# Causal masks carried in the shift operands, expert tables worked out in PSUM, and matmuls of zeros at the start

## The chip, the cores and the metric

One core of a Trainium2 chip runs the whole program. Five engines take instructions in their own order: PE (TensorE: matmuls, with weight loads listed apart as PEld), DVE (VectorE), ACT (ScalarE), POOL (GpSimd) and SP, which here only starts DMAs. The metric is the device time of one execution in microseconds (us). "Granted clock" is the share of full speed at which TensorE was let run: 1.00 is 2.4 GHz, 0.50 is 1.2 GHz.

## The reference

Attention with a decay, and then a layer of eight experts of which each token takes one:

```python
# q, k, v: 8 batches x 8 heads x 576 positions x 64; f: 8 x 8 x 576
scores = matmul(q, k.T) / sqrt(64)
cum = cumsum(log(clip(f, 1e-4, 1)), axis=-1)
scores = where(causal, -1e9, scores + cum[..., :, None] - cum[..., None, :])
attn = exp(scores - scores.max(-1));  attn /= attn.sum(-1) + 1e-9
x = matmul(attn, v)                       # as 4608 tokens x 512
logits = x @ w_gate + modality_bias[modality_id]
e = argmax(logits); gate = softmax(logits)[e]
out = gate * (relu(x @ w1[e]) @ w2[e])    # w1: 8 x 512 x 1024, w2: 8 x 1024 x 512
```

## The kernel before

**Attention** runs over 32 pairs of heads (four pairs are one batch). A pair lies in one tile `X` (two heads of 64 partitions each), as a rounded part `X[:,0]` and the rest `X[:,1]`, so that a product is three matmuls. The two heads of a pair use the upper and the lower 64 rows of the PE array; each matmul of a group therefore comes twice. The steps of pair p, by the names that the planner uses:

- `mm(p,g)` (`max_mm`, L525 on): query by key scores from the rounded parts alone, into one of three PSUM buffers `ps`. A bf16 matmul adds the decay of the key (`Cq` by `Sk`, L546), and ahead of it small matmuls of an identity (`id2`) by a triangle of minus 1e30 (`after`, L540) mask the blocks on the diagonal. `mr(p,g)` on DVE takes the row maxima; `sp`, `ssp` and `so` turn them round on PE, split them on DVE and put them, negated, as rows of `Sq` by two DMAs of SP (L586).
- `s(p,g)` (`scores`, L589 on): the scores proper, keys on the partitions. Mask matmuls again (`id2` by `later`, L606), then the shift (`Sk` by `Sq`, bf16, L613: minus the maximum of the query, plus the decay), then three matmuls of `X` (L621). `e` (exp) and `h` (rounding) are ACT's, `r` (the rest, L663) POOL's and DVE's.
- `w(u)`, `d(u)` for head u: attention by v (L689 to L691), and the division on DVE. `kg` (L491) is the gate's product with v.
- `hi`, `lo` split X on ACT and POOL; `cum` (L412) copies the three bf16 parts of the pair's decay into rows of `Sk` by one DMA of SP. `Sk`, `Sq` and `X` have three slots, which pairs take in turn.

**Routing** per batch (`rt`, `sc`): argmax, ranks within the experts, and scatter of the tokens with indirect DMAs to lists in DRAM. After batch 5, `early` (L1327) counts the tokens per expert so far, and works out on DVE, with 25 small instructions, nearly all on SBUF tiles of one partition (L1000 to L1074), which expert the first four tiles of 256 tokens belong to, so that their loads can start before attention ends.

**The experts** (`Moe.run`) take 18 tiles of 256 tokens and a few of 128, PE without a break; the other tables are worked out by `other_tables` in the middle of the third tile.

**The order** in attention is written down by a planner: `Plan.order` takes, among the steps that are ready and whose buffers are free, the one of the least due time; due times are 43.41 us per batch and a table `DUE` of offsets by step, stage (first, second, middle, last batch) and pair. Each engine then runs its instructions strictly in that order.

**The start** (`setup`): constants on DVE and POOL, the decay's sum (`chl`, three bf16 parts), the first two pairs' loads. `setup2` makes the constants for routing.

Of the kernel before, what the change touches and what calls it, by code (L numbers as in the profile page):

```python
# [24 lines left out]
S = 576  # L25
# [30 lines left out]
BIG = 1.0e30  # L56
# [5 lines left out]
def f32(ap):  # L62
# [6 lines left out]
    ('setup2',): ((-7.6276,),), ('gs',): ((-27.0565,),),  # L69
    ('hi',): ((-64.9614, -0.5129, 9.9233, 25.1464,), (-37.0423, -34.3266, 3.0090, 3.2864,), (-169.6259, -130.5347, 3.9150, -109.9118,), (-15.1432, -125.2677, 14.8978, 18.2475,),),  # L70
    ('lo',): ((-30.4199, -46.7722, 10.3081, -40.1680,), (-2.3325, -25.1233, 8.8097, -14.1207,), (-7.8613, -11.7188, 13.3481, 20.8245,), (-10.1281, -19.8797, 18.8280, 34.3170,),),
    ('cum',): ((-242.6133, -50.2149, -6.6544, -25.4361,), (-56.0267, -77.1295, -25.7943, 18.3990,), (-19.3542, -20.5147, -34.8776, -48.3972,), (-31.7442, -27.2763, -26.2392, 12.4635,),),
# [8 lines left out]
    ('ssp',): ((-1.1033, 5.5259, 26.1725, 29.0023,), (8.9962, 9.7417, -25.8497, 38.9986,), (0.8838, 13.9798, 19.4950, 37.8791,), (11.5482, 4.7540, 36.4772, 37.2843,),),  # L81
# [1396 lines left out]
```

## Time and profile before

| what | value |
|---|---|
| three runs, median (lowest to highest) | 850.12 us (849.7 to 854.04) |
| the profiled execution | 849.61 us, its span from first to last instruction 847.8 us |
| PE busy over the span | 807.1 us (95%) |
| attention, about 0 to 376 us; experts, about 376 to 848 us | |

The profile comes from one execution. A busy engine is one with an instruction in flight; for PE, whose matmuls are pipelined, the distance from the start of one group of matmuls to the start of the next is the better measure of what a group costs. A wait is put down to the instruction whose end released it.

### The profile page before, as it was taken

How to read it: one execution, taken by the hardware profiler on the slowest of the kernel's cores; microseconds unless marked ns; L12 is line 12 of the kernel's file. 1: busy time of each engine (PE TensorE's matmuls, PEld its weight loads, DVE VectorE, ACT ScalarE, POOL GpSimd, SP SyncE). 2: the span in 40 equal slices, each digit the busy share in tenths (PEclk: the TensorE clock that was granted, in tenths of full speed). 3: DMA queues.
4: the chain of work that ended last, by engine and by line, in shares of the span. 5: the costliest groups of instructions: out<-in, count | busy, mean ns of one | idle time of the engine just before them, and what ended most of it. 6: DMA issues, size and time to landing. Idle time of an engine off the chain costs nothing.

```text
span 847.8 us, 23444 instructions
## 1 busy us (share of the span) xinstructions
PE 807.1 (95%) x9693; PEld 726.9 (86%) x9693; DVE 627.7 (74%) x1170; ACT 543.2 (64%) x688; POOL 378.7 (45%) x370
## 2 busy tenths in 40 slices
PE   3899999999999999699999999999999999999994
PEld 2689898989898988588999999999999999999873
DVE  8679798989898989877777856666655666566484
ACT  4597889898989897474643654444454445444484
POOL 9386889898989897575433111111000110111110
PEclk9699999999999999899999999999999999999997
DMA  5434353535353533171474731101113421116481
GB/s 171 145 104 140 125 182 116 184 116 180 119 182 116 184 115 108 64 244 58 149 249 157 295 121 51 51 27 49 38 51 137 149 67 50 51 44 207 146 299 30
DMA packets 43016, 107.48 MB, mean 127 GB/s; under 512 B 5391, under 2 KB 5583, under 8 KB 42896
## 3 DMA queue, kind: packets, MB, share of 16 engines
q1 hardware_dynamic: 36192, 84.82, 30.1%
q0 software_dynamic: 6704, 21.02, 6.8%
q8 instruction: 80, 1.31, 0.7%
q14 instruction: 40, 0.33, 0.1%
HBM read 143.14 MB, written 21.80 MB: 195 GB/s over the span
## 4 chain that ended last, share of the span: by engine, by line
PE 86%; DVE 7%; POOL 2%; issue 2%; ACT 1%; DMA 0%; DVEq 0%; POOLq 0%; ACTq 0%
PE ph L1211 23%; PE py L1237 23%; PE ps L621 9%; PE pb L491 4%; PE po L689 4%; PE po L691 3%; PE po L690 3%; PE ps L551 3%; PE ps L613 3%; PE ps L546 2%; PE ph L1293 2%; PE ps L606 2%; PE px L1194 2%; PE ps L540 2%; DVE w1l L1157 1%
## 5 line engine op out<-in xcount | busy, mean ns | idle before, releaser
L1242 POOL DMA_INDIRECT out_dram<-y,xg x36 | 48.0, 1334 | 333.7 <-DVE y L1241 304.8
L1211 PE MATMUL ph<-xh,w1h 128*128 128x256 f32 x576 | 163.3, 284 | 0.3 <-DVE hl L1215 0.3
L1211 PE MATMUL ph<-xl,w1h 128*128 128x256 f32 x576 | 163.1, 283 | 0.0
L1211 PE MATMUL ph<-xh,w1l 128*128 128x256 f32 x576 | 162.9, 283 | 0.0
L663 POOL TENSOR_TENSOR Pl<-Pt,Ph 128x1024 f16<-128x1024 f32 (+1 forms) x63 | 142.0, 2260 | 17.9 <-ACT Ph L651 14.4
L1157 DVE TENSOR_TENSOR w1l<-raw,w1h 128x1024 fp32r<-128x1024 f32 x78 | 97.6, 1265 | 61.5 <-ACT w1h L1155 61.5
L1174 ACT CAST w2h<-raw 128x1024 fp32r<-128x1024 f32 x72 | 74.6, 1048 | 95.1 <-issue 55.3
L1155 ACT CAST w1h<-raw 128x1024 fp32r<-128x1024 f32 x80 | 82.5, 1048 | 82.5 <-PE ph L1211 62.5
L1175 DVE TENSOR_TENSOR w2l<-raw,w2h 128x1024 fp32r<-128x1024 f32 x72 | 87.5, 1221 | 58.7 <-ACT w2h L1174 56.9
L1211 PEld LDWEIGHTS ph<-xh,w1h 128*128 128x128 f32 x576 | 110.5, 192 | 1.2 <-DVE hl L1215 0.5
L1237 PE MATMUL py<-w2h,hh 128*128 128x512 f32 x288 | 111.3, 395 | 0.0
L1211 PEld LDWEIGHTS ph<-xl,w1h 128*128 128x128 f32 x576 | 110.5, 192 | 0.7
L1211 PEld LDWEIGHTS ph<-xh,w1l 128*128 128x128 f32 x576 | 110.5, 192 | 0.0
L1237 PE MATMUL py<-w2l,hh 128*128 128x512 f32 x288 | 110.2, 391 | 0.0
L1237 PE MATMUL py<-w2h,hl 128*128 128x512 f32 x288 | 109.9, 391 | 0.0
L621 PE MATMUL ps<-X 64*128 64x288 f32 (+4 forms) x1152 | 109.8, 319 | 0.0
L689 PE MATMUL po<-vh,Ph 128*128 128x73 f16 x930 | 100.3, 199 | 2.1 <-DVE lgh L705 2.1
L403 POOL TENSOR_TENSOR X<-raw,X 128x1152 fp32r<-128x1152 f32 x32 | 84.7, 2649 | 38.5 <-ACT X L397 38.2
L691 PE MATMUL po<-vh,Pl 128*128 128x73 f16 x930 | 99.8, 198 | 1.5 <-DVE Pl L663 1.3
L690 PE MATMUL po<-vl,Ph 128*128 128x72 f16 x930 | 100.1, 196 | 0.0
L689 PEld LDWEIGHTS <-Ph 128*128 128x128 f16 x960 | 93.6, 98 | 5.9 <-issue 2.8
L636 ACT ACTIVATE Pt<-ps,lnp 128x576 f32<-128x576 f32 (+1 forms) x96 | 81.3, 864 | 24.9 <-PE ps L621 24.9
(301 smaller groups left out, 1944.2 us busy)
## 6 DMA issues: line engine op xcount, KB each, us to landing
raw<-in_w_dram SPq DMA_DIRECT2D x84, 1024.0 KB
raw<-in_qk_dram SPq DMA_DIRECT2D x32, 608.0 KB
vT<-in_vt_dram SPq DMA_DIRECT2D x32, 320.0 KB
xg<-xs SPq DMA_DIRECT2D x18, 514.0 KB
vr<-in_v_dram SPq DMA_DIRECT2D x30, 256.0 KB
raw1b<-in_w_dram SPq DMA_DIRECT2D x4, 1024.0 KB
hxg<-xs SPq DMA_DIRECT2D x5, 257.0 KB
vr<-in_v_dram SPq DMA_DIRECT2D x8, 128.0 KB
```

The lines of the kernel that those rows point to most:

```text
L403: e.tensor_tensor(self.two(X[:, 1]), self.two(self.get("raw", p)), self.two(f32(X[:, 0])), ALU.subtract)
L621: nc.tensor.matmul(ps[:, h, c0:c0 + w], X[r, x, k], X[r, y, q], start=False, stop=(j == 2), skip_group_check=True)
L636: nc.scalar.activation(self.get("Pt", (p, i))[:, :, o:o + w], ps[:, :, 0:w], AF.Exp, bias=self.lnp, scale=0.125)
L663: e.tensor_tensor(self.Pl_t[p % 2][:, :, c], self.exps(p, i), self.Ph_t[p % 2][:, :, c], ALU.subtract)
L689: nc.tensor.matmul(o, Ph[:, c0:c0 + P], vh[:, c, hh, :], start=(c == 0), stop=False)
L690: nc.tensor.matmul(o[:, 1:73], Ph[:, c0:c0 + P], vl[:, c, hh, :], start=False, stop=False)
L691: nc.tensor.matmul(o, Pl[:, c0:c0 + P], vh[:, c, hh, :], start=False, stop=(c == ic))
L1155: x = nc.scalar.copy(self.w1h[a], self.raw1[i][a])
L1157: y = e.tensor_tensor(self.w1l[a], self.raw1[i][a], f32(self.w1h[a]), ALU.subtract)
L1175: y = nc.vector.tensor_tensor(self.w2l[a], self.raw2[a], f32(self.w2h[a]), ALU.subtract)
L1211: y = nc.tensor.matmul(ph[:, i, :], w[:, k, f0:f0 + P], x[:, k, :], start=(j == 0), stop=(j == len(m) - 1))
L1237: x = nc.tensor.matmul(py, h[:, k, c * P:c * P + P], w[:, k, :], start=(j == 0), stop=(j == len(m) - 1))
```

## The change

- **Masks.** The mask matmuls go, with `id2`, `after` and `later`. The shift matmuls carry the mask in rows of their operands that were empty: `Sk` has three variants per slot (no mask, and one for each half of a diagonal block), `Cq` too, and `Sq` holds a staircase (`ques`) next to the shift's rows. A shift matmul over a diagonal block is cut into pieces of 64 columns, each with its variant.
- **The decay's rows** go to three variants, so `cum` is now two DMAs of SP (one per head), read from a copy in DRAM (`sums`) that SP writes once; for pair 0 it is six DMAs, three on ACT's queue. The operands of slots 1 and 2 are filled by two new steps, `slot`, on ACT and POOL.
- **Early tables.** They are worked out in the PSUM bank of the counts, in two pieces with a DVE step of routing between, and with fewer instructions; the count of what is done (four instructions) moves to `other_tables` in the source. The loads that follow are a step of their own, `early3`.
- **Zeros.** 24 matmuls of 512 columns of zeros stand ahead of the first step, and 56 of 256 columns behind nine of the first steps. They write a PSUM bank that the first `w` takes over.
- **Order and constants.** A new `DUE` table, planner's costs for `mm` and `s` lowered, `setup2` cut in three, and the constants of the experts moved from the program's start behind it.

```diff
-BIG = 1.0e30
+BEFORE = (24, 512)
+BETWEEN = {('gs',): 16, ('mm', 0, 2): 5, ('mm', 0, 1): 10, ('mm', 1, 2): 7, ('v1', 0): 3, ('v3', 0): 2, ('s', 0, 2): 7, ('kg', 0, 1): 3,
+           ('mm', 2, 2): 3}
+MLOW, MTOP = 2.0 ** -43, 2.0 ** 36
...
-    ('setup2',): ((-7.6276,),), ('gs',): ((-27.0565,),),
+    ('slot',): ((0.0000, -90.2608, -60.5121,),), ('setup2',): ((-42.1805,),), ('setup3',): ((-15.4352,),),
...
+        self.idle = self.new(self.ps_o, "po", -1, [P, 512], F32, 1)
+        self.turn_over(*BEFORE)
...
+    def rows(self, copy, i):
+        copy(self.Sk[:, i].rearrange("p v (c n) -> p v c n", n=P),
+             self.keys.rearrange("p v (o n) -> p v o n", o=1).broadcast_to([P, 3, NJ, P]))
...
     def put_cum(self, p):
 
         self.own(("cum", p % 3), p)
-        self.nc.sync.dma_start(self.Sk[3:114:22, p % 3, 0:S], self.chl[2 * p:2 * p + 2])
+        for h, e in enumerate((self.nc.sync, self.nc.scalar if p == 0 else self.nc.sync)):
+            o, u = self.Sk[64 * h + 3:64 * h + 6, p % 3, :, 0:S], 2 * p + h
+            if p:
+                e.dma_start(o, self.sums[u].rearrange("r (o s) -> r o s", o=1).broadcast_to([3, 3, S]))
+            else:
+                for v in range(3):
+                    e.dma_start(o[:, v], self.chl[u:u + 1])
+        if p == 0:
+            self.nc.sync.dma_start(self.sums, self.chl)
...
+    def parted(c0, w, ic, j0):
+
+        if j0 + w != MW[ic]:
+            return [(c0, w, ic, j0, 0, 0)]
+        e = w - 64
+        r = [(c0 + e, 64, ic, j0 + e, 1, 2)]
+        if w > 64:
+            r = [(c0 + e - 64, 64, ic, j0 + e - 64, 2, 1)] + r
+        return ([(c0, w - P, ic, j0, 0, 0)] if w > P else []) + r
...
-                    nc.tensor.matmul(ps[:, h, c0:c0 + n], self.id2[r, x], self.later[r, x, 0:n], start=first, stop=False,
-                                     skip_group_check=True)
-                first = False
+        parts = []
         for c0, w, c, i0 in segs:
+            n = 0
+            if i0 == P * c:
+                n = min(w, P)
+                parts += [(c0 + 64 * a, 64, c, i0 + 64 * a, 1 + a) for a in range(n // 64)]
+            if w > n:
+                parts.append((c0 + n, w - n, c, i0 + n, 0))
+        for n, (c0, w, c, i0, v) in enumerate(parts):
...
-            add("early", (), [("PE", 0.2), ("POOL", 0.15), ("DVE", 4.5), ("SP", 2.3)], 0, early, (), [("sc", EB, c) for c in range(NJ)], take=("pb", "e"), free=[("pb", "e")])
+            add("early", (), "PE", 0.25, self.begin_early, (early,), [("setup4",), ("rt", EB, 4)], take=("pb", "e"))
+            add("early1", (), "DVE", 2.0, self.go_early, (), [("early",)])
+            add("early2", (), "DVE", 1.8, self.go_early, (), [("early1",)], free=[("pb", "e")])
+            add("early3", (), "SP", 2.3, self.load_early, (), [("early2",)] + [("sc", EB, c) for c in range(NJ)])
...
+    def turn_over(self, n, w):
+
+        for _ in range(n):
+            self.nc.tensor.matmul(self.idle[:, 0:w], self.none[:, 0:P], self.none[:, 0:w], start=True, stop=True)
...
             for s in self.steps(early).order():
                 s["fn"]()
+                self.turn_over(BETWEEN.get(s["name"], 0), 256)
```

PE in the steady part, one group of scores `s(p,0)` (288 columns, of which the first 128 lie on the diagonal). Before, `id` by `later` is the mask and `Sk` by `Sq` the shift:

```order
L606 LDWEIGHTS id_173
L606 MATMUL ps<-later,id_173 128x128
...
L606 MATMUL ps<-later,id_173 128x64
...
L613 LDWEIGHTS Sk
L613 MATMUL ps<-Sq,Sk 128x288
...
L621 MATMUL ps<-X_117 128x288 x6
```

Two mask blocks (192 columns per head) stand ahead of one shift of 288. PE in the same group in the changed kernel:

```order
L646 LDWEIGHTS Sk
L646 MATMUL ps<-Sq,Sk 128x64
...
L646 MATMUL ps<-Sq,Sk 128x64
...
L646 MATMUL ps<-Sq,Sk 128x160
...
L654 MATMUL ps<-X_101 128x288 x6
```

The mask's columns are gone; the shift's 288 columns come as 64, 64 and 160, each with its own weights.

DVE at the early tables before (`c_na` are the counts, `c_ea` and `c_ka` the expert and the place of each tile, `c_taba` the table, `pb` a PSUM bank):

```order
L739 TENSOR_REDUCE rei<-rc 128x5
L1000 COPY c_na<-pb 1x8
L1007 TENSOR_SCALAR c_nia<-c_na 1x8
...
L1026 TENSOR_TENSOR c_lea<-c_cuma,c_io 1x32
...
L1059 CAST c_taba<-c_cuma 1x1
...
L1072 TENSOR_SCALAR c_done<-c_done 1x8
L1073 TENSOR_TENSOR c_done<-c_done,c_nta 1x8
L1074 TENSOR_SCALAR c_done<-c_done 1x8
L663 TENSOR_TENSOR Pl_214<-ps,Ph_212 128x2x512
L561 TENSOR_REDUCE mt<-ps 128x2 x2
```

The rest of the exponentials (L663) and the next maxima (L561) stand behind the whole chain. DVE at the same place in the changed kernel:

```order
L1405 CAST pb<-pb 1x8
L1406 TENSOR_SCALAR pb<-pb 1x8
...
L1416 TENSOR_TENSOR c_le_8474<-pb,c_io 1x32
...
L772 TENSOR_REDUCE rei<-rc 128x5
L1421 TENSOR_TENSOR c_le_8475<-c_io,pb 1x4
...
L1433 COPY c_early<-pb 1x16
L1130 TENSOR_TENSOR c_done<-c_early 1x8
L1131 TENSOR_SCALAR c_done<-c_done 1x8
...
L595 TENSOR_REDUCE mt<-ps 128x2 x2
L696 TENSOR_TENSOR Pl_212<-ps,Ph_210 128x2x512
```

Every instruction of the tables has a PSUM operand; routing's minimum (L772) now stands in the middle. In the order that results the four instructions of `c_done` (on SBUF) still stand at this place, ahead of the maxima (L595), which now come before the rest (L696).

PE at the start before (`gmax` is the gate's scale, then the first maxima of pair 0):

```order
L467 MATMUL pb<-ident,gmax 1x128
L470 MATMUL pb<-gmax_232,ones_209 128x1
L540 LDWEIGHTS id_173
L540 MATMUL ps<-after,id_173 128x64
...
L546 MATMUL ps<-Sk,Cq 128x64
```

PE starts with two small matmuls and goes on to the first pair. PE at the start of the changed kernel (`none` is the tile of zeros):

```order
L947 LDWEIGHTS none
L947 MATMUL po<-none 128x512
...
L498 MATMUL pb<-ident,gmax 1x128
L501 MATMUL pb<-gmax_265,ones_224 128x1
L947 LDWEIGHTS none
L947 MATMUL po<-none 128x256
...
L569 MATMUL ps<-Sk,Cq 128x64
```

24 matmuls of zeros stand ahead of the first step and 16 narrower ones between it and the first pair; the steps themselves keep their order here.

## Rows read from the trace of the kernel before

**Rows 1.** Stages: us, busy of PE, PEld, DVE, ACT, POOL, PEclk, DMA share, GB/s.
```profile
60.00:304.00 244.00, 242.34 (x4872) 218.78 (x4869) 211.54 (x524) 213.51 (x276) 205.14 (x179) 1.00 0.46 148
304.00:376.00 72.00, 63.56 (x1274) 56.73 (x1272) 58.69 (x151) 53.63 (x67) 53.60 (x56) 0.95 0.36 121
376.00:848.00 472.00, 459.15 (x2960) 416.31 (x2956) 313.02 (x397) 236.71 (x295) 80.47 (x79) 0.99 0.33 114
```
**Rows 2.** Waits from 60 to 304 us: total, times, longest.
```profile
ACT ps L630 <- PE ps L621: 12.8, 17, 1.2
ACT Pt L636 <- PE ps L621: 11.7, 17, 1.8
```
**Rows 3.** Timeline of PE, one pair's matmuls: start us, us, engine, line, operands, count.
```profile
282.10 0.34 PE L540 MATMUL ps<-after,id 64*128 64x128 bf16 x8
282.28 0.38 PE L546 MATMUL ps<-Sk,Cq 64*128 64x192 bf16 x4
...
285.07 0.26 PE L606 MATMUL ps<-later,id 64*128 64x128 bf16 x4
285.17 0.29 PE L613 MATMUL ps<-Sq,Sk 64*128 64x288 bf16 x2
...
286.36 0.29 PE L606 MATMUL ps<-later,id 64*128 64x128 bf16 x6
286.48 0.38 PE L613 MATMUL ps<-Sq,Sk 64*128 64x448 bf16 x4
```
**Rows 4.** Groups by line on PE, 60 to 304 us: count, busy us, mean ns.
```profile
L606 PE MATMUL ps<-later,id 64*128 64x64 bf16 (+1 forms) x410 | 20.3, 205 | 0.0
```
**Rows 5.** Stages at the start, as in rows 1.
```profile
21.00:24.00 3.00, 0.86 (x7) 0.24 (x3) 2.79 (x7) 0.00 (x0) 3.00 (x2) 0.85 0.00 1
...
30.00:33.00 3.00, 3.00 (x26) 2.63 (x26) 2.46 (x5) 1.28 (x2) 0.00 (x0) 0.50 0.38 104
39.00:42.00 3.00, 2.08 (x32) 1.46 (x28) 2.75 (x5) 3.00 (x5) 3.00 (x2) 1.00 0.79 277
```
**Rows 6.** Timeline at the start: loads on SP, work on DVE, then PE.
```profile
0.82 0.61 SPq L247 DMA_DIRECT2D Pt<-in_f_dram  x1
...
3.68 0.73 DVE L274 TENSOR_SCALAR Pt<-Pt 64x576 f32<-64x576 f32 x1 [0.83 <-DMA Pt<-in_f_dram]
...
13.72 0.37 PE L467 MATMUL pb<-ident,gmax 128*1 128x128 f32 x1 [13.72 <-POOL vh L329]
...
27.25 0.38 PE L606 MATMUL ps<-later,id 64*128 64x128 bf16 x4
```
**Rows 7.** Timeline of PE, the end of the first pair's scores.
```profile
38.06 0.34 PE L540 MATMUL ps<-after,id 64*128 64x128 bf16 x8
```
**Rows 8.** Timeline at the early tables, DVE and POOL.
```profile
340.03 0.14 DVE L1000 COPY c_na<-pb 1x8 f32<-1x8 f32 x1
340.21 0.88 DVE L1007 TENSOR_SCALAR c_nia<-c_na 1x8 int32<-1x8 f32 x1
...
341.65 2.63 POOL L403 TENSOR_TENSOR X<-raw,X 128x1152 fp32r<-128x1152 f32 x1
...
341.79 2.53 DVE L1026 TENSOR_TENSOR c_lea<-c_cuma,c_io 1x32 f32<-1x32 f32 x1
...
346.32 2.32 DVE L1072 TENSOR_SCALAR c_done<-c_done 1x8 f32<-1x8 f32 x1
...
348.95 1.23 DVE L663 TENSOR_TENSOR Pl<-ps,Ph 128x1024 f16<-128x1024 f32 x1
```
**Rows 9.** Timeline of PE behind the early tables.
```profile
350.23 0.50 PE L606 MATMUL ps<-later,id 64*128 64x128 bf16 x8 [4.98 <-DVE Pl L663]
```
**Rows 10.** The stage behind the early tables, as in rows 1.
```profile
350.00:355.00 5.00, 4.53 (x54) 3.54 (x54) 3.19 (x12) 2.16 (x2) 0.33 (x2) 0.58 0.23 82
```
**Rows 11.** Timeline of SP's queue in the steady part.
```profile
66.49 0.67 SPq L412 DMA_DIRECT2D Sk<-chl  x1
67.95 1.21 SPq L586 DMA_DIRECT2D Sq<-mT  x2
```

More of the change, by code (lines that the diff above doesn't have):

```diff
@@ L292, in setup @@
-        mask(self.after, 1)
+        self.queries(nc.gpsimd.tensor_copy, 0)
+        self.Ph_t = [t([P, 2, PW], F16, f"Ph{i}") for i in range(2)]
+        self.Pl_t = [t([P, 2, PW], F16, f"Pl{i}") for i in range(2)]
+        for x in self.vh:
+            nc.gpsimd.memset(x[:, :, :, 0:1], 1.0)
+            nc.gpsimd.memset(x[64:128, 4, :, 0:1], 0.0)
+        for x in self.Ph_t + self.Pl_t:
+            nc.gpsimd.memset(x[:, :, 1600:], 0.0)
         nc.scalar.activation(ft, ft, AF.Ln)
+        self.rows(nc.scalar.copy, 0)
@@ L304, in setup @@
         nc.scalar.activation(one, one, AF.Exp)
[L305 to L310 removed]
+        for x in self.X3:
+            nc.vector.memset(f32(x[:, :, S:QC]), 0.0)
         nc.sync.dma_start(self.idt, ids.bitcast(I32).rearrange("p (n o) -> p n o", o=2))
@@ L933, in __init__, with constants @@
         nc = self.nc
+        self.xg, self.xh, self.xl = {}, {}, {}
+        self.xgh, self.xhh, self.xlh = {}, {}, {}
+        self.rings, self.used = {}, {}
+        self.ring("xg", keep, 3, [P, 2, 514], F32)
+    def constants(self):
+        nc, keep = self.nc, self.keep
         self.ident = keep.tile([P, P], F32, name="cident")
@@ L947, in __init__ @@
         self.gap = keep.tile([1, 1], I32, name="c_gap")
-        self.xg, self.xh, self.xl = {}, {}, {}
-        self.xgh, self.xhh, self.xlh = {}, {}, {}
-        self.rings, self.used = {}, {}
-        self.ring("xg", keep, 3, [P, 2, 514], F32)
+        self.zeros = keep.tile([1, 8], F32, name="c_zeros")
+        nc.gpsimd.memset(self.zeros, 0.0)
     def ring(self, name, pool, n, shape, dt):
@@ L1327, in early, with t @@
     def early(self, acc, pc):
-        self.first_table(self.counts(acc, pc, "a"))
-        for t in range(2):
-            self.load_x(t)
+        self.nc.tensor.matmul(pc[:, 0:8], self.ones, acc, start=True, stop=True)
+        yield
+        vec = self.nc.vector
+        at = 8
+        def t(*shape):
+            nonlocal at
+            n = int(np.prod(shape))
+            at += n
+            x = pc[0:1, at - n:at]
+            if len(shape) == 1:
+                return x
+            return x.rearrange("o (a b) -> o a b", b=shape[1])
@@ new lines, in early @@
+        keep = self.keep.tile([1, 16], F32, name="c_early")
+        s1, s3 = [1, EARLY, 1], [1, EARLY, 8]
+        ni = t(8).bitcast(I32)
+        vec.tensor_copy(ni, pc[0:1, 0:8])
+        vec.tensor_scalar(ni, ni, 8, None, ALU.arith_shift_right)
+        e = t(EARLY + 1, 1)
+        vec.memset(e[:, 0:1], -1.0)
+        at_nt = at
+        nt, cum = t(8), t(1, 8)
+        vec.tensor_copy(nt, ni)
+        vec.tensor_tensor_scan(cum[:, 0], nt, self.zeros, 0.0, ALU.add, ALU.add)
+        io = self.io[:, 0:EARLY]
@@ new lines, in early @@
+        base, k = t(EARLY, 1), t(EARLY, 1)
+        le, left = (self.keep.tile([1, EARLY, n], F32, name=f"c_le{n}") for n in (8, 1))
+        vec.tensor_tensor(le, cum.broadcast_to(s3), io.broadcast_to(s3), ALU.is_le)
+        vec.tensor_reduce(e[:, 1:], le, AX.X, ALU.add)
+        vec.tensor_tensor(le, le, cum.broadcast_to(s3), ALU.mult)
+        vec.tensor_reduce(base, le, AX.X, ALU.max)
+        yield
+        vec.tensor_tensor(left, io, base, ALU.subtract)
+        vec.scalar_tensor_tensor(k, e[:, 1:], float(CAP // T), left, ALU.mult, ALU.add)
@@ L1333, in run @@
+        vec.tensor_copy(keep[:, 0:16], pc[0:1, at_nt:at_nt + 16])
+        self.row = [tab[0:1, :, i:i + 1] for i in range(EARLY)]
+        self.last = ex[:, EARLY:EARLY + 1]
+        self.early_counts = keep
+        yield
+        for i in range(2):
+            self.load_x(i)
+        yield
     def run(self, acc, loads, behind, ahead, ranks):
```

297 lines of the change are left out of this document (154 added, 143 removed), and 54 rows, old and new, of the table DUE.

## The prediction

> **What bounds the kernel now.** I read the stages first, then the waits, the matmuls of one pair in the timeline, and last the two places where PE stands still. The stages [rows 1] show that from 60 to 304 us PE is busy for 242.3 of 244.0 us at full clock, while ACT (213.5), DVE (211.5) and POOL (205.1) have an eighth or more to spare. The longest waits of ACT in that stretch end with PE's scores, 12.8 and 11.7 us [rows 2]. So in the middle of attention PE's stream of matmuls is the bound, and a microsecond taken out of it is a microsecond gained until another engine is full. From 304 to 376 us PE is busy for 63.6 of 72 us only: the longest hole is a wait of 4.98 us that ends with DVE's L663 [rows 9]. At the start PE runs, once it has work, at half clock: 0.50 from 30 to 33 us [rows 5]. From 376 us on the experts keep PE at 459.2 of 472 us, and there the order of the instructions is what it was; I put no change there.
>
> **Masks, what goes.** In one pair there are six groups of mask matmuls, three in the maxima (6, 8 and 4 instructions) and three in the scores (4, 6 and 8). Start to start up to the shift that follows, 8 take 282.28 - 282.10 = 0.18 us, 4 take 0.10 and 6 take 0.12 [rows 3]. That is 0.40 us in the maxima and 0.40 in the scores, 0.80 us per pair. For a check: the groups hold 2 x 832 columns per head, both heads at once, and 1664 / 2.4 GHz is 0.69 us.
>
> **Masks, what comes.** The shift's columns stay as they are, but a diagonal block is cut: 28 pieces per head and pair stand where there were 12, and 18 more of them than before are 64 columns wide. No group of before holds such pieces with the shift's own weights. The mask groups are the nearest: they took 0.80 us for 0.69 us of columns, 0.11 us over, and if that lies with their ten pieces of 64 columns, it is 0.01 us each. 18 x 0.01 = 0.18, which leaves 0.80 - 0.18 = 0.62 us gained per pair, and this value I take. The ends: pieces that cost nothing give 0.80. Pieces that cost a slot each, whatever their width, give 32 added matmuls (16 pieces, two heads) at 0.18 / 8 = 0.022 us, 0.70 us, and leave 0.10.
>
> **How much of it reaches the end.** There are 410 of the scores' mask matmuls between 60 and 304 us [rows 4], 18 per pair: 23 pairs. 23 x 0.62 = 14.3 us. That stretch would then take 230 us, with ACT at 93% and DVE at 92%; both wait for PE now and will wait less, and the first time that one of them is late PE waits in turn. I take nine tenths, 12.8 us (ends: 45%, if ACT and DVE can't be packed so close, and all). The other nine pairs, 5.6 us, run at the start and the end of attention, where other waits set the pace: half, 2.8 us.
>
> **The decay's rows.** One DMA of SP with 0.67 us of issue [rows 11] becomes two per pair. What stands behind them on SP, the next `so` (1.21 us for two) and the loads, starts up to 0.7 us later. `mm` waits for these rows. In the new order the first maxima of every fourth pair stand before a gate product and a group of scores instead of behind them, with `so` and then `cum` on SP ahead: about 1 us on DVE, 1.2 and 1.3 us of issue, and a landing for which the only read row is the first load (issued from 0.82 to 1.43 us, its user starts at 3.68 [rows 6]), 2.25 us. 5.8 us in sum. Between lie the last scores of the pair before, two heads of attention by v and two groups of maxima; by a pair's 244.0 / 23 = 10.6 us I estimate them at 6 us. So it is covered, narrowly, and I cost it at nothing; uncovered it is a fraction of a microsecond in every fourth pair.
>
> **Early tables.** From the first copy (340.03) to L663 (348.95) DVE is 8.9 us on them. Three instructions on SBUF tiles take 0.88, 2.53 and 2.32 us, against 0.14 us for the copy out of PSUM. L1026 ends as POOL's subtraction that began at 341.65 does, 2.63 us later [rows 8]. So it is POOL that they wait for, some 5.3 us in all; the other 22 instructions take the remaining 3.2 us, 0.145 each. In the changed kernel 18 instructions with a PSUM operand take their place. [...]
>
> But in the order that results, the four instructions of `c_done`, still on SBUF, stand at the same place, ahead of the maxima. Of the waits 0.7 and 2.4 us go; the third (about 2.2) may meet POOL anywhere in a subtraction, half of it on the mean. 23 instructions (the 18, the four, and a copy of the last expert) at 0.145 us, 0.2 for routing's minimum and 1.1 of waiting give 4.6 us instead of 8.9: 4.3 us less. Behind the hole the clock was 0.58 on the mean from 350 to 355 us [rows 10], with 4.5 us of work: about 1.9 us lost, of which a shorter hole gives back perhaps half. What is late next is step 4 of routing, which PE now meets before the last scores of its pair; I take 0.7 us off for it. Sum: 4.3 + 0.9 - 0.7 = 4.5 us (ends 2 and 7).
>
> **The start.** The first pair's scores and two gate products run from 27.25 to 38.06 us [rows 6, 7] at a clock of 0.50; at full clock a stream of matmuls would take half, 5.4 us less. Before that PE was nearly idle (0.86 of 3 us from 21 to 24 us, clock 0.85 and falling [rows 5]). The zeros fill such waits. 40 matmuls of 256 columns stand between the pairs; 256 columns at 2.4 GHz are 0.11 us, 4.3 us together, and PE has to do them in order even when its next step is ready. The waits of before cover most of that. ACT takes over as the bound from 39 us on, where it is busy for 3.00 of 3 us [rows 5], but its work starts earlier too. The first matmul of a step stood at 13.72 us [rows 6]; with six DMAs for the first rows, three of them behind ACT's table load, I leave the first maxima where they are. I take 4.5 us (ends 0, if zeros and ACT eat it, and 6).
>
> [...]
>
> **Sum.** 12.8 + 2.8 + 4.5 + 4.5 = 24.6 us. The profiled execution took 849.6 us, near the median of 850.1; 849.6 - 24.6 = 825.0 us.
>
> **Rivals.** (a) ACT and DVE become the bound: for it speaks that ACT is at 88% and DVE at 87% now, with dependent steps on a ring of three PSUM buffers; against it, that most of their idle time is waiting for PE. Then 45% of the steady gain is had, 6.4 us, of the edges 1.4, of the start 4.5 and of the tables 4.5: 849.6 - 16.8 = 832.8. (b) The matmul's slot, not its columns, is what is paid: 0.10 us per pair, 23 x 0.10 + 0.4 = 2.7, with start and tables 849.6 - 11.7 = 837.9. Eight mask matmuls in 0.18 us speak against more than 0.022 each. [...] (c) The zeros don't hold the clock up, or stand in the way: the start gives nothing, 829.5; it lies within the forecast's range. (d) Slower: the decay's rows, now through DRAM and on two DMAs behind `so`, land behind the time at which PE comes to the maxima. PE's order is fixed, so all later pairs wait. It decides from 24.6 / 32 = 0.77 us per pair on; at 1.2 us per pair in every pair the sum is 38 - 25 = 13 us the wrong way, 863 us. For it speaks the narrow cover above, against it that it is narrow in one pair of four. (e) The change doesn't do what it says: the mask's columns cannot come back, as the instructions are gone; only the clock can fail, which is (c).
>
> **Chances.** Forecast with (c) 75%, (a) 13%, (b) 6%, (d) 4%; 2% are left for a change that ends near nothing. What a measurement of this kernel can tell from no change is about 0.5%, 4.2 us. Faster 0.94, same 0.02, slower 0.04. Range: with 0.80 us in all 32 pairs, 6 and 7 us it would be 811; with (b) 838. 811 to 838 holds the forecast and (a); the likeliest case alone is 815 to 832.
>
> **What would show it.** Right: no mask line; from 60 us on about 40.2 us per batch instead of 42.4 (four pairs of 10.6, less 0.9 x 0.62 each), PE still at 97% or more; granted clock near 1.00 from 15 us on; DVE's tables below 6 us and PE's hole behind them at most 3 us. Wrong: PE with waits for ACT or DVE in every batch (a); shift groups longer by the full slot (b); PE waiting for DMAs at the first maxima (d).

## The result, and the profile after

In runs side by side the changed kernel took 840.46 us (838.6 to 842.75), the kernel before 851.51: a ratio of 0.987, 95% interval 0.983 to 0.991. That is 11 us less, where 24.6 were forecast; the range began at 811 and ended at 838. In a second block the two took 839.1 and 846.6 us, 7.4 us less (the row "again" of the table below). The profiled execution took 840.2 us, its span is 838.2 (before: 847.8), 9.6 us less.

Three matmuls divide both spans: the shift's transpose of the fourth pair, that of the 28th, and the first matmul of the experts. First the timeline of PE of the kernel before (start us, us, engine, line, operands, count):

```profile
53.97 0.28 PE L572 MATMUL pb<-ident,mt 128*10 128x128 f32 x1
...
307.59 0.28 PE L572 MATMUL pb<-ident,mt 128*10 128x128 f32 x1
...
377.19 0.36 PE L1211 MATMUL ph<-xh,w1h 128*128 128x256 f32 x1
```

Then the changed kernel:

```profile
48.20 0.28 PE L606 MATMUL pb<-ident,mt 128*10 128x128 f32 x1
...
299.98 0.28 PE L606 MATMUL pb<-ident,mt 128*10 128x128 f32 x1
...
367.61 0.36 PE L1271 MATMUL ph<-xh,w1h 128*128 128x256 f32 x1
```

The start gained 53.97 - 48.20 = 5.8 us. The 24 pairs between took 253.6 and now 251.8, 1.8 less. From there to the experts it was 69.6 and is 67.6, 2.0 less. The experts take 470.6 us in both. In the trace of again, the changed kernel once more, the three are 48.2, 251.6 and 66.3 us. So the start came near its term, the tail gave 2.0 to 3.3 of its 4.5 us, and the steady part, for which 12.8 and part of 2.8 us were put down, gave 1.8 to 2.0.

The stages, as in [rows 1] (us, busy of PE, PEld, DVE, ACT, POOL, PEclk, DMA share, GB/s):

```profile
60.00:304.00 244.00, 240.23 (x4871) 215.33 (x4869) 215.59 (x528) 217.24 (x281) 208.96 (x187) 1.00 0.45 149
304.00:376.00 72.00, 64.50 (x1180) 58.56 (x1179) 54.60 (x146) 49.79 (x62) 52.77 (x50) 0.95 0.39 135
```

PE is still busy for 98.5% of the steady part: its idle time grew from 1.7 to 3.8 us. DVE and ACT are busy for 4 us more than before. ACT's waits for PE's scores are hardly shorter than in [rows 2], and PE's own wait for DVE, once in a batch, is longer (total us, times, longest; ACT's in the changed kernel, then PE's in the kernel before and in the changed one):

```profile
ACT Pt L669 <- PE ps L654: 12.0, 18, 1.4
ACT ps L663 <- PE ps L654: 10.9, 17, 1.1
```

```profile
PE po L689 <- DVE lgh L705: 1.7, 5, 0.3
```

```profile
PE pb L481 <- DVE a L475: 3.3, 5, 0.8
```

What the masks left is read best where both kernels have the same six groups in a row, four of scores and two of maxima, and then the transpose. The kernel before, the first rows and the last of such a stretch:

```profile
210.10 0.26 PE L606 MATMUL ps<-later,id 64*128 64x128 bf16 x4
...
210.72 0.30 PE L613 MATMUL ps<-Sq,Sk 64*128 64x288 bf16 x2
...
211.25 0.34 PE L540 MATMUL ps<-after,id 64*128 64x128 bf16 x8
...
215.14 0.28 PE L572 MATMUL pb<-ident,mt 128*10 128x128 f32 x1
```

The changed kernel, the first row of each group:

```profile
286.77 0.30 PE L646 MATMUL ps<-Sq,Sk 64*128 64x64 bf16 x6
...
287.36 0.29 PE L646 MATMUL ps<-Sq,Sk 64*128 64x288 bf16 x2
...
287.89 0.40 PE L569 MATMUL ps<-Sk,Cq 64*128 64x64 bf16 x12
...
288.48 0.40 PE L646 MATMUL ps<-Sq,Sk 64*128 64x64 bf16 x8
...
289.67 0.40 PE L569 MATMUL ps<-Sk,Cq 64*128 64x64 bf16 x8
...
290.30 0.40 PE L646 MATMUL ps<-Sq,Sk 64*128 64x64 bf16 x12
...
291.47 0.28 PE L606 MATMUL pb<-ident,mt 128*10 128x128 f32 x1
```

5.04 us became 4.70. The last groups of maxima take 0.27 and 0.35 us in both kernels, so a pair is 0.34 us cheaper on PE, not 0.62. The second group of each stretch has no block on the diagonal: 288 columns of shift alone, 0.53 us in both. The first has the same shift with masks, 0.62 us, and as pieces of 64, 64 and 160, 0.59 (0.58 in most).

Of these 4 x 0.34 = 1.4 us per batch only 0.4 arrive: from the transpose of one batch to that of the next it is 42.2 us before and 41.8 now. PE's busy time in it fell by 0.8 us, from 41.9 to 41.1, and its idle time rose by 0.4, from 0.3 to 0.7 or 0.8 (means of three batches, the changed kernel in two traces). So some 0.5 us went to the new order of PE's work, and 0.4 to waits.

### The profile page after: what moved, and what is told of

The parts are those of the page before. It is cut to its first block, busy times and chain, and to the rows that moved or that the text cites. A ratio compares the mean times of both kernels' runs of the same rounds, so it can differ in the third digit from the quotient of the medians.

```text
span 838.2 us, 23454 instructions
## 1 busy us (share of the span) xinstructions
PE 808.4 (96%) x9645; PEld 720.8 (86%) x9645; DVE 620.6 (74%) x1178; ACT 546.8 (65%) x691; POOL 384.1 (46%) x376
## 3 DMA queue, kind: packets, MB, share of 16 engines
q8 instruction: 79, 1.29, 0.7%
## 4 chain that ended last, share of the span: by engine, by line
PE 89%; DVE 7%; issue 2%; ACT 2%; DMA 0%; ACTq 0%; DVEq 0%
PE ph L1271 24%; PE py L1297 23%; PE ps L654 9%; PE po L722 4%; PE pb L522 4%; PE ps L574 4%; PE po L724 4%; PE po L723 3%; PE ps L646 3%; PE ps L569 3%; PE ph L1353 2%; PE px L1254 2%; DVE mt L595 1%; PE pb L606 1%; DVE w1l L1217 1%
## 5 line engine op out<-in xcount | busy, mean ns | idle before, releaser
L696 POOL TENSOR_TENSOR Pl<-Pt,Ph 128x1024 f16<-128x1024 f32 (+1 forms) x63 | 142.4, 2267 | 17.3 <-ACT Ph L684 16.4
L1217 DVE TENSOR_TENSOR w1l<-raw,w1h 128x1024 fp32r<-128x1024 f32 x78 | 95.2, 1234 | 60.2 <-ACT w1h L1215 60.2
L654 PE MATMUL ps<-X 64*128 64x288 f32 (+4 forms) x1152 | 108.1, 316 | 0.0
L722 PE MATMUL po<-vh,Ph 128*128 128x73 f16 x930 | 100.4, 198 | 1.4 <-DVE lgh L738 1.4
L722 PEld LDWEIGHTS <-Ph 128*128 128x128 f16 x960 | 93.6, 98 | 7.3 <-issue 2.5
L723 PEld LDWEIGHTS <-Ph 128*128 128x128 f16 x960 | 94.6, 99 | 0.8 <-issue 0.5
```

What stands on the lines that cost most here:

```text
L654: nc.tensor.matmul(ps[:, h, c0:c0 + w], X[r, x, k], X[r, y, q], start=False, stop=(j == 2), skip_group_check=True)
L696: e.tensor_tensor(self.Pl_t[p % 2][:, :, c], self.exps(p, i), self.Ph_t[p % 2][:, :, c], ALU.subtract)
L722: nc.tensor.matmul(o, Ph[:, c0:c0 + P], vh[:, c, hh, :], start=(c == 0), stop=False)
L723: nc.tensor.matmul(o[:, 1:73], Ph[:, c0:c0 + P], vl[:, c, hh, :], start=False, stop=False)
L1217: y = e.tensor_tensor(self.w1l[a], self.raw1[i][a], f32(self.w1h[a]), ALU.subtract)
```

## The experiments

"First matmul" is that of the experts, from each trace; what follows it takes 470 to 472 us. The last two columns are from the transpose of pair 16 to that of pair 18 (the two pairs around v's scale) and from there to pair 20. Medians of one block were taken on one chip, with the kernel before beside them.

| kernel | median us | before | ratio, 95% | first matmul | two pairs | next two |
|---|---|---|---|---|---|---|
| before | | | | 377.2 | 23.4 | 18.8 |
| changed | 840.5 | 851.5 | 0.983 to 0.991 | 367.6 | 22.3 | 19.5 |
| p32 | 847.9 | 849.2 | 0.997 to 1.002 | 374.9 | 22.6 | 20.3 |
| wide | 842.8 | 849.2 | 0.989 to 0.995 | 370.5 | 22.2 | 19.7 |
| order | 883.9 | 849.2 | 1.036 to 1.044 | 415.4 | 29.6 | 20.4 |
| nozeros | 841.0 | 849.2 | 0.986 to 0.994 | 370.6 | 22.2 | 19.5 |
| oldorder | 864.5 | 852.3 | 1.008 to 1.021 | 391.2 | 23.6 | 18.4 |
| v2b | 858.9 | 852.3 | 1.003 to 1.011 | 387.9 | 26.3 | 19.5 |
| merged | 838.2 | 852.3 | 0.978 to 0.989 | 366.6 | 22.4 | 19.4 |
| done | 836.2 | 852.3 | 0.976 to 0.988 | 364.6 | 22.3 | 19.5 |
| again | 839.1 | 846.6 | 0.988 to 0.992 | 366.1 | 22.3 | 19.5 |
| nozeros2 | 842.4 | 846.6 | 0.990 to 0.995 | 370.3 | 22.2 | 19.5 |
| dlater | 839.0 | 846.6 | 0.988 to 0.993 | 366.7 | 22.2 | 19.5 |
| best | 834.4 | 846.6 | 0.982 to 0.987 | 359.3 | 22.3 | 19.4 |
| dve_v | 839.2 | 852.5 | 0.982 to 0.989 | 366.8 | 22.3 | 19.5 |
| dve_o | 839.3 | 852.5 | 0.982 to 0.988 | 368.5 | 22.6 | 19.5 |
| spread | 854.0 | 852.5 | 1.000 to 1.004 | 377.2 | 22.1 | 22.9 |
| best2 | 850.3 | 852.5 | 0.996 to 1.000 | 375.9 | 21.8 | 21.6 |
| bestagain | 835.1 | 852.1 | 0.978 to 0.984 | 362.3 | 22.4 | 19.4 |
| best3 | 854.8 | 852.1 | 1.002 to 1.007 | 382.9 | 21.7 | 24.3 |

**The price of a piece: p32, wide, merged.** p32 cuts each 64-column piece once more, wide halves the wide ones; both use this, p32 with `v > 0`:

```diff
+        segs = [(c0 + a, b, ic, j0 + a, v, q) for c0, w, ic, j0, v, q in segs for a, b in halves(w, w >= 160)]
         for n, (c0, w, ic, j0, v, q) in enumerate(segs):
```

> The changed kernel with each of the 18 pieces of 64 columns (per head and pair) cut once more, into two of 32: the columns and the result stay, 36 matmuls per pair are added. Theory A (a matmul of the shift has a slot of about 22 ns, as 0.18 us for eight mask matmuls, so two heads' pieces take 45 ns or their columns, whichever is longer): 18 x 45 ns = 0.81 us more per pair, 32 pairs, 26 us: about 866. Rival B (each cut costs a small fixed amount, 13 ns per added matmul, from 0.80 - 0.34 us per pair that the steps of the two kernels show): 36 x 0.013 = 0.47 per pair, 15 us: about 855. Rival C (pieces cost their columns alone, and the missing gain went elsewhere, to the new order and to other engines): no change, 840.

> The changed kernel with the uncut pieces of 160 columns and more halved (8 per head and pair, into halves of 80 to 160 columns): 16 matmuls per pair are added, the columns and the result stay. Theory A (slot of 22 ns per matmul, hidden where two heads' columns take longer than 45 ns): halves of 80 and 96 columns take 33 and 40 ns of columns, so 2 x 23 + 2 x 10 ns = 0.07 us per pair, 2 us: about 842. Rival B (13 ns for every added matmul): 0.21 per pair, 6.7 us: about 847. Rival C (columns alone): 840.

The same six groups in p32, first and last row:

```profile
208.99 0.34 PE L652 MATMUL ps<-Sq,Sk 64*128 64x32 bf16 x10
...
214.03 0.28 PE L611 MATMUL pb<-ident,mt 128*10 128x128 f32 x1
```

5.04 us instead of 4.70: 32 added matmuls cost 0.34 us, 10.6 ns each, so B's size (0.013), half of A's, and not C's nothing. The total grew by 7.4 us where B had 15: the two pairs around v's scale took only 0.3 us more, the next two the full 0.8.

That is the price of going from 64 columns to 32, and not that of the cut itself. From the start of one head's matmul and its neighbour beside it to the start of the next two, the traces have 25 ns at 32 columns, 29 at 64, 57 at 128, 84 at 192 and 137 at 320: two pieces of 32 take 50 ns where one of 64 took 29, but two of 64 take 58 where one of 128 takes 57. The last two shift matmuls of a group are another matter: the first matmul of X starts 25 to 30 ns behind them whatever their width, from 32 to 448 columns (39 ns where they are the only ones). wide shows the difference; the first two of the six groups in its trace, and the start of the third:

```profile
288.17 0.30 PE L652 MATMUL ps<-Sq,Sk 64*128 64x64 bf16 x8
...
288.78 0.30 PE L652 MATMUL ps<-Sq,Sk 64*128 64x144 bf16 x4
...
289.37 0.41 PE L574 MATMUL ps<-Sk,Cq 64*128 64x64 bf16 x14
```

The second group, whose only piece was halved, takes 0.59 instead of 0.53 us; the first, whose last piece of 160 was, 0.61 instead of 0.59. Where a piece of 160 to 320 columns with narrow ones behind it was halved, a group takes 0.00 to 0.01 us more. So wide's 2.3 us more lie between A and B, but neither has its reason.

For two heads' matmuls side by side hardly anything is saved by width from 64 columns down to 32: 29 ns at 64 and 25 at 32.

merged puts the two 64-column pieces of a group that have the same weights into one matmul:

```diff
+        alike = {}
+        for y in segs:
+            alike.setdefault(y[5] or ("whole", y[0]), []).append(y)
...
+                    o, i = blocks(pm[:, h, 0:512], c0, c1), blocks(self.Sk[r, p % 3, v, 0:576], j0, j1)
```

> The changed kernel, in which pieces of the maxima with the same weights are one matmul over two blocks of 64 columns (three per head and pair go: 6 matmuls fewer per pair, the same columns). By the 10.6 ns that each added matmul took in p32's steps: 0.064 us per pair, 2 us: about 838.5. By a slot of 22 ns: 0.11 per pair, 3.5 us: 837. If a matmul over two blocks is slower than two of one block: 840 or more.

Two groups of maxima have merged pieces. In order of time, each with the start of the group behind it:

```profile
288.08 0.40 PE L578 MATMUL ps<-Sk,Cq 64*128 64x64 bf16 x8
...
288.61 0.40 PE L654 MATMUL ps<-Sq,Sk 64*128 64x64 bf16 x8
...
289.78 0.40 PE L578 MATMUL ps<-Sk,Cq 64*128 64x128 bf16 x6
...
290.41 0.40 PE L654 MATMUL ps<-Sq,Sk 64*128 64x64 bf16 x12
```

The group with twelve shift matmuls has eight now and takes 0.53 instead of 0.59 us. The one with eight has six and takes 0.63 us as before. The edit also changed the order of the pieces: in the first group the widest one, of 192 columns, now comes last; in the second a piece of 64 still does. By the starts above, 192 columns take 84 ns inside a group and 28 at its end. The difference is the gain, so it lies in the order and not in the merging, as far as these two groups show. No run changed the order alone. The pairs that PE sets got it (19.4 for 19.5 us); the two around v's scale did not, and the first matmul of the experts, 366.6, lies between the changed kernel's two traces (367.6 and 366.1). The total decides nothing, and 0.06 us per pair came as written down, but not by 10.6 ns per matmul.

**The zeros: nozeros, nozeros2** (`BEFORE = (0, 512)`, `BETWEEN = {}`).

> The changed kernel without the matmuls of zeros, ahead of the first pairs and between their steps. Theory A (the zeros hold the clock up at the start): the first pairs run at half clock again as before (0.50 from 24 to 37 us), about 5 us more: 845. Rival B (zeros give nothing, the start's gain is from the other loads and the order): 840. Rival C (they cost more than they give): 837.

> The kernel without zeros once more, beside the changed kernel. In its first trace the transpose of the fourth pair stands at 53.7 us instead of 48.2 and that of the last at 352.7 instead of 348.4, but its median was 841.0. Theory A (the zeros' 4 us at the end of attention reach the end): 3 to 5 us above the kernel again. Rival B (experts or the hole behind the early tables take it back): the same within 1 us.

The median of the first, 841.0, spoke for B, its trace for A; with the changed kernel beside it the second took 3.2 us more, and both traces reach the experts 3 to 4 us later. Theory A, somewhat smaller. The first gate product in nozeros2, then in the kernel again:

```profile
27.67 2.31 PE L521 MATMUL pb<-gv,vT 128*128 128x16 f32 x10
```

```profile
26.89 1.29 PE L522 MATMUL pb<-gv,vT 128*128 128x16 f32 x10
```

The same ten matmuls take 2.31 and 1.29 us: half speed without zeros, as before [rows 5]. In nozeros the second gate product, at 36.7 us, still takes 2.31 us; in nozeros2, at 35.9 us, it takes 1.29. (The clock's column says 1.00 in both, but nozeros2's trace has no entry for the clock ahead of 35.0 us; the durations are what to go by.) The transpose of the fourth pair stands at 53.7 and 51.0 us in the two traces without zeros, 54.0 before and 48.2 with them: half to nearly all of the start's gain is the zeros'.

**The order: order, v2b, oldorder.** Numbers of the table alone; order has the first three lines, v2b the first and the last, oldorder the kernel before's numbers for batches 1 to 6.

```diff
-    ('v2',): (..., (1.3830,), ...            +    ('v2',): (..., (2.2000,), ...
-    ('mm', 1): (..., (0.7747, ...            +    ('mm', 1): (..., (2.4000, ...
-    ('sp',): (..., (9.2313, 15.7400, 27.2300, 38.0838,)
+    ('sp',): (..., (11.1500, 16.9000, 27.2300, 41.1000,)
-    ('kg', 0): (..., (6.2968,), ...          +    ('kg', 0): (..., (7.6000,), ...
```

> The changed kernel with four numbers of its table altered for batches 2 to 6: v's scale (L481) goes behind the product by v that stood behind it, ahead of one group of maxima, and the shift's transpose (L606) behind the last scores in three pairs of four, next to a product by v. Theory A (the new order takes back part of what the masks give: the wait of PE at L481, 0.9 us in three batches of four, and a transpose between two groups of scores, 0.2 us each): five batches by 0.7 + 3 x 0.2 us, 6 us less: about 834 (ends 832 and 838, if something else is late next). Rival B (all of the missing gain is the pieces' price; the order costs nothing, as other waits fill the same time): 840. Slower, 843, if the later transpose makes the next scores late.

> The changed kernel with two numbers of its table altered: in batches 2 to 6 v's scale (L481) goes behind the second product by v instead of ahead of it, the gate's first product (L522) behind one group of scores. The shift's transpose stays where it was. Theory A (PE's wait of 0.8 us at L481 in each batch is on the path): five batches by 0.8 us, 4 us: about 836. Rival B (it is late for DVE whatever stands there; the wait goes to the next step that needs DVE): 840. Rival C (as a later transpose did, a later scale makes v's split and the gate late): above 844, with PE waiting for ACT.

> The changed kernel with the table's numbers of the kernel before for batches 1 to 6 (all but the loads and the decay's rows): there PE's order is the old one, with the new operands, zeros and early tables. Theory A (the pieces leave 0.34 us per pair of the masks' gain, and the new order gives most of it back): a batch of four pairs takes 42.24 - 1.36 = 40.9 us instead of 41.9, six batches 6 us: about 834. Rival B (with cheaper maxima and scores the next chain is bound, whatever the order): as it is, 840. Rival C (the new order is there because the decay's rows and the shift, now with more on SP's queue, come later): PE waits for DMAs, clock falls at the waits: slower than 846.

All three got slower than the changed kernel, by 18 to 43 us, far more than any case written down. The cases for slower had the direction, but only order's had the wait: in v2b PE waited for DVE and not for ACT, and in oldorder the longest wait is one of 6.6 us for DVE's maxima, against 1.4 us for DMAs. PE's waits from 60 to 330 us in v2b:

```profile
PE pb L606 <- DVE vl L534: 5.4, 4, 1.5
PE ps L646 <- DVE ps L597: 4.2, 5, 0.8
PE po L722 <- DVE a L475: 3.1, 5, 0.8
```

and in order, from 60 to 304 us, the longest two:

```profile
PE ps L646 <- DMA Sq<-mT: 9.8, 4, 3.7
PE ps L569 <- DVE mt L595: 5.6, 4, 1.4
```

A transpose one group of scores later made the shift's DMA late; PE stood, the clock fell (0.91 from 100 to 300 us, against 1.00), and behind several of the waits PE ran at half speed: the gate's product at 155 us took 2.31 us instead of 1.29. So the transposes among the scores, which cost 0.2 us each, can't go one group later as things are; order moved v's scale too, and no run moved the transposes alone. In oldorder the pairs off v's scale take 18.4 instead of 18.8 us, and PE's busy time there is 18.3 instead of 18.8: with the order of before 0.5 of the 0.68 us of two pairs arrive. But the two pairs around v's scale take 23.6, and two seams to the other batches cost some 10 us each (pair 4 to 5: 23.7 us instead of 13.4). It does not show what the old order would give with numbers of its own.

**The early tables: done.**

```diff
-        vec.tensor_tensor(done, cum, nt, ALU.subtract)
+        self.order(vec.tensor_tensor(done, cum, nt, ALU.subtract), self.low)
```

> The changed kernel with the four instructions of c_done held behind attention (in order of DVE behind the last pair's work), out of the hole of PE behind the early tables. Theory A (they stand 3.0 us ahead of the maxima's reduction there, 2.5 of it a wait for POOL, and PE waits for that): 2 to 3 us: about 838, and the first expert instruction as much earlier. Rival B (the next instruction of DVE meets POOL in the same way, or PE is late there for another reason): 840.

In the changed kernel the tables take 6.0 us on DVE instead of 8.9 [rows 8], and one instruction still waits for POOL; DVE, POOL, then PE:

```profile
332.10 0.15 DVE L1405 CAST pb<-pb 1x8 int32<-1x8 f32 x1
...
335.68 2.49 DVE L1133 TENSOR_SCALAR c_done<-c_done 1x8 f32<-1x8 f32 x1
338.09 1.27 DVE L595 TENSOR_REDUCE mt<-ps 128x2 f32<-128x128 f32 x2
```

```profile
335.51 2.64 POOL L426 TENSOR_TENSOR X<-raw,X 128x1152 fp32r<-128x1152 f32 x1
```

```profile
339.41 0.27 PE L606 MATMUL pb<-ident,mt 128*10 128x128 f32 x1 [1.69 <-DVE mt L595]
```

In done the reduction follows the last copy of the tables with no such wait:

```profile
335.52 0.15 DVE L1433 COPY c_early<-pb 1x16 f32<-1x16 f32 x1
336.35 1.29 DVE L595 TENSOR_REDUCE mt<-ps 128x2 f32<-128x128 f32 x2 [0.68 <-PE ps L574]
```

PE's wait there goes from 1.7 to 0.4 us and the experts begin at 364.6 instead of 366.1 to 367.6. Theory A, 1.5 to 3 us. From the transpose of the 28th pair to the experts it is 60.6 to 63.9 us in the five traces with this edit, and 65.3 to 68.9 in the thirteen others of the changed kernel and its variants, oldorder left out.

**What sets the two pairs around v's scale: dlater, dve_v, dve_o, spread, best2, best3.** Busy times in the two halves of the fifth batch, columns as above; the kernel before, then the changed one:

```profile
181.50:204.90 23.40, 23.06 (x456) 20.63 (x454) 21.24 (x52) 20.12 (x24) 20.71 (x19) 1.00 0.38 123
204.90:223.80 18.90, 18.90 (x397) 17.22 (x393) 15.48 (x41) 17.12 (x25) 16.00 (x16) 1.00 0.59 183
```

```profile
174.40:196.70 22.30, 21.52 (x425) 19.00 (x423) 20.61 (x51) 19.32 (x24) 19.53 (x17) 1.00 0.41 138
196.70:216.20 19.50, 19.50 (x410) 17.69 (x408) 16.51 (x42) 18.00 (x25) 17.29 (x18) 1.00 0.53 168
```

In the second half PE never stands; in the first it does, with DVE at 91% before and 92% now. dlater takes the row in front of the copy that PE waits for:

```diff
-    ('d', 1): (..., (32.5008, 17.8069, ...     +    ('d', 1): (..., (32.5008, 43.7100, ...
```

> The changed kernel with one number of its table altered: in batches 2 to 6 DVE's division by sums (L733 to L738, 1.1 us) of the product in front goes behind the copy of v's maximum (L475) instead of ahead of it. PE's order stays. Theory A (PE waits 0.8 us a batch at L481 because that copy is queued behind the division): the wait goes, five batches by 0.8 us, up to 4 us less than the kernel again. Rival B (the division is then late for the next product by v, which waits for its PSUM buffer): the same, with a wait at L722.

Rival B, nearly: the wait at L481 is gone (3.3 to 0.2 us) and the time is the same. PE's waits in dlater:

```profile
PE pb L522 <- DVE mT L613: 1.4, 4, 0.5
PE po L722 <- DVE lgh L738: 1.3, 5, 0.3
```

dve_v and dve_o add an instruction of DVE in one half or the other (measured: 0.68 us):

```diff
+                if s["name"] in EXTRA:    # ("v2", b), or ("sp", 4 * b + 2)
+                    self.nc.vector.tensor_reduce(self.scrap, self.none, AX.X, ALU.max)
```

> The changed kernel with one more instruction of DVE in batches 2 to 6, a reduction of 128x512 zeros to one column (some 0.6 us, by the 0.76 us that 576 columns take), behind v's scale, in the two pairs of a batch in which DVE was busy for 20.6 to 21.2 of 22.3 us. Theory A (DVE sets the time there: those two pairs took 22.2 to 22.4 us in seven kernels whose PE work differs): they take 22.8 to 22.9 us, five batches, 3 us: about 843, and the first matmul of the experts at 370 us. Rival B (PE sets the time there too): 840, 367 us.

> The same instruction of DVE in the other two pairs of batches 2 to 6, behind the shift's transpose of the third pair, where PE is busy for 19.5 of 19.5 us and DVE for 16.4. Theory A (PE sets the time there): no change, 19.5 us, 840. Rival (DVE's latency, and not its busy time, is what PE waits for, in any place): 0.6 us a batch, 843.

dve_v refuted A as I had put it: 0.68 us more of DVE's work behind v's scale changed nothing. The wait at L481 lies ahead of it and may make PE late enough to cover it; that is a reading, no run shows it. dve_o cost nothing where it stood, as A had it, but 0.3 us in the two pairs that follow. The remaining three take work of DVE out of the first half:

```diff
-    ('vl', 0): (..., (8.6766,), ...     +    ('vl', 0): (..., (17.3000,), ...   # best3: 21.2
-    ('vl', 3): (..., (6.8403,), ...     +    ('vl', 3): (..., (19.0000,), ...   # not in best3
```

> The changed kernel with two numbers altered: of the four splits of v that DVE does in a row (L548, 3.25 us) in batches 2 to 6 two go behind the division of the pair after, out of the two pairs in which DVE is full into the two in which it has 3 us to spare. Theory A (DVE sets the time of the first two pairs): 22.3 goes down to about 21.8, where PE's own work is the bound; 5 batches by 0.5, 2 to 4 us: about 837. Rival B (it was PE, or the chain of dependent steps): 840. Rival C (the split is late for the product by v of the next batch): slower, PE waiting at L722.

> The same two numbers on top of the kernel with merged pieces, c_done behind attention and the later division (834.4 beside 839.1 of the changed kernel): with DVE relieved, PE's shorter maxima and the missing wait at L481 count: 21.3 us for the first two pairs instead of 22.25, five batches, 4 us less: about 830. If the two pairs stay at 22.25, it was not DVE: 834.

> The same with one of DVE's splits of v (0.8 us) in batches 2 to 6 behind the routing of the batch before, where DVE stood idle for 0.4 us, and so behind the maxima that PE's PSUM buffers waited for when two splits were moved. Theory A (in the first two pairs DVE's row of instructions is what PE waits for at L522): 22.3 goes to 21.9, the other two pairs stay at 19.4: 2 us less than its neighbour, 831. Rival B (any DVE work in the other pairs makes the maxima late there): the third pair gets longer by 0.5 us or more: 834 or above.

In the halves they relieve, all three went the way that A says, if not by as much: 22.3 became 22.1, 21.8 and 21.7 us, the first times that these pairs moved below 22.2. The other half paid more, so the totals are 17 to 24 us above what A named. C of spread and B of best3 had the direction, but not the wait: spread's PE waits for DVE's maxima at L646 (8.4 us), and best3's longest waits stand one pair behind the third. The two halves in best, then in best3:

```profile
173.50:195.80 22.30, 21.54 (x412) 18.86 (x410) 21.19 (x51) 19.11 (x24) 19.92 (x19) 1.00 0.44 142
195.80:215.20 19.40, 19.40 (x399) 17.61 (x397) 16.20 (x42) 18.05 (x25) 16.42 (x16) 1.00 0.51 166
```

```profile
184.70:206.40 21.70, 21.32 (x413) 18.83 (x411) 20.02 (x50) 19.23 (x24) 18.16 (x16) 1.00 0.38 127
206.40:230.60 24.20, 21.10 (x398) 18.91 (x396) 17.22 (x43) 18.07 (x25) 17.64 (x18) 0.93 0.48 150
```

In best DVE is busy for 21.2 of 22.3 us, and PE waits for it behind the splits. In best3 DVE has 20.0, PE 21.3 of 21.7. PE's wait from 60 to 304 us, in best and in best3 (there once, in another half):

```profile
PE pb L522 <- DVE mT L621: 1.7, 4, 0.5
```

```profile
PE pb L522 <- DVE mT L621: 0.5, 1, 0.5
```

Up to 10.6 us into the half the two kernels stand alike, with the same 0.34 us of waiting at L730. The shorter time lies behind it, where the split was taken out: the gate's product of L522 starts at 15.25 us in best and at 14.63 in best3. In spread it does not: there the wait at L481 got shorter, 0.76 to 0.56 us, which stands 7 us ahead of the splits. So best2 and best3 show DVE's row as the bound, and spread does not. But 0.8 us of DVE's work in a half with 3 us to spare made PE wait there, 9.3 us in all:

```profile
PE ps L578 <- DVE Pl L704: 9.3, 4, 3.2
```

**A faster version: again, best, bestagain.** best is merged, done and dlater together.

> The changed kernel itself once more, as the neighbour of the next three on one chip: 838 to 842.

> The changed kernel with the three edits together: merged pieces of the maxima (2 us), c_done behind attention (3 to 4 us), the division behind the copy (0 to 4 us): 5 to 9 us less than the kernel again, about 833.

> The kernel with the three edits (merged pieces, c_done behind attention, the division behind the copy of v's maximum) once more, beside the next one: 832 to 835.

834.4 beside 839.1 us, and 835.1 in another block: 4 to 5 us below the changed kernel and 1.6 to 1.9% below the one before, the fastest of all. Most of it lies behind the 28th pair, where done's edit is; 4.7 us is just short of the 5 to 9 written down.

## Why the prediction was wrong, point by point

**The step that failed is "How much of it reaches the end", nine tenths of 0.62 us per pair.** Measured: 0.34 us per pair saved on PE, and 1.8 us over 24 pairs, 0.08 each, at the end. Three things lie in it: the pieces cost more than their term, the new order of PE's work took 0.5 us of each batch, and waits for DVE 0.4.

**The term for what comes: 18 x 0.01 = 0.18 us for the pieces.** The gain is 0.34 us, not 0.62. The masks' own cost isn't measured over a whole pair; four of them take 0.085 us by whole groups with and without, where the starts that I read gave 0.10. Between their columns (0.69; by the starts above 128 columns more, from 192 to 320, take 53 ns, so 1664 take 0.69 us) and their starts (0.80) it leaves 0.35 to 0.46 us for the pieces, at least twice the term. I had priced each piece alike. The traces show that it matters where it stands: four added matmuls cost 0.05 us where a piece of 160 columns stays last (0.53 and 0.58 us) and 0.085 where one of 64 comes last (the third group of maxima, 0.27 us without a block on the diagonal, 0.355 as 160, 64 and 64, and 0.354 with masks before: nothing gained). Before, a shift of 192 to 448 columns stood last in nearly every group, and most of it cost nothing by itself. By this alone 23 x 0.34 x 0.9 = 7.0 us would stand where 12.8 stood.

**An order costed at nothing.** I worked out waits for the new order, but no price on PE. In both traces a group of scores or maxima is 0.09 us longer when something other than a product on 64 rows follows (1.08 and 1.17 us for the same group of twelve shift matmuls and twelve of X). The new order has twelve such places in a batch, the old one ten: 0.2 us. Three transposes stand among scores instead of one, 0.2 us to the next start instead of 0.1 where a product by v follows: another 0.2 us. That is most of the 0.5 us per batch by which PE's busy time fell short of what the steps give. The half of a batch that PE sets went from 18.8 to 19.5 us, though its groups got cheaper; part of that is work that moved between halves, as the other half got 1.1 us shorter. The runs show that the transposes and v's scale can't simply go back (order, v2b), not that no better order exists.

**The nine tenths.** I had reasoned with DVE at 92% over 230 us. That mean hid two halves of a batch: in the two pairs around v's scale DVE is at 92 to 95% and PE waits for it, once at L481, or, where that wait was taken away, at L522 and L722. There eight kernels took 22.2 to 22.4 us, with PE busy for 21.5 to 21.8; p32, with PE busy for 22.2, took 22.6. That is rival (a), but in half of the pairs and with DVE alone; ACT was never what PE waited for there. That DVE's row is the bound is shown by taking work out (21.8 and 21.7 us, best2 and best3), not by adding it (dve_v). It took 0.4 us per batch, the growth of PE's waits; so rival (a) is a part of the miss, and not the largest.

**What held.** The decay's rows: PE waited for no DMA at the maxima in the changed kernel, rival (d) did not occur. The start: 5.8 us for 4.5, of which leaving out the zeros takes 3 to 4 at the end, so (c) falls. The early tables: the 18 instructions with a PSUM operand took 0.15 us each on the mean, where 0.145 was counted; DVE's part went from 8.9 to 6.0 us, with the wait for POOL inside `c_done` that I had expected by half and that came whole (2.49); 2.0 to 3.3 us arrived instead of 4.5, and done got 1.5 to 3 more. Rival (b) named 837.9 and came nearest by luck: its 0.10 us per pair is near the 0.08 that was left at the end, but the pieces left 0.34 on PE.

Open: what PE's order would have to be for DVE's 37 us per batch of 42 to spread evenly. It wasn't found in the six tries here. Open too is what the pieces of before and now would cost with the widest one last in every group.

## What to carry to other kernels

Read an engine's share per stretch of the period, not over the whole stage: a mean of 87% hid a half at 91 to 95% in which PE waited for DVE. When columns are traded for more and narrower matmuls, price each by whole groups, with and without the cut, and look at which piece comes last: here cutting that one cost 0.04 to 0.05 us, cutting others 0.01 or less, and from 64 columns down to 32 width saves hardly anything (29 and 25 ns). And in an order this tight a step that moves can cost far more than it was meant to save (best3: 20 us for 2), as the clock can fall with the stalls (0.93 in best3's longer half, 0.91 over 200 us in order).

## What the runs showed of the hardware

- Two heads' bf16 matmuls side by side, on 64 rows each and with weights loaded each time, hold the next two back by 25 ns at 32 columns, 29 at 64, 57 at 128, 84 at 192 and 137 at 320. The last two ahead of X's matmuls hold those back by only 25 to 30 ns at any width from 32 to 448 (X then took 0.02 us longer at 320 columns, 0.08 at 448).
- From matmuls on 64 rows to ones on 128 PE loses 0.09 us: the next start comes 112 or 204 ns behind the last matmul of X in the kernel before, 113 or 204 in the changed one. No run here varied the rows by themselves.
- With stalls of one to four microseconds in each batch the granted clock was 0.91 over 200 us (order, longest wait 3.7 us; 1.00 in the changed kernel), and behind several of them the same work took nearly twice as long (a gate product 2.31 us instead of 1.29).
- Ten matmuls of 256 columns of zeros in a row take 2.34 us at a granted clock of 0.50 and 1.26 at 1.00 (changed kernel, from 13.78 and 19.53 us), 213 and 109 ns from start to start: 1.2 and 2.35 columns per ns. The forecast's 0.11 us for 256 columns at 2.4 GHz is borne out by the second.
